# Infini-attention with a channel MLP on one core: the memory read as two 64-row products, dimensions as rows

## The chip, the cores and the metric

The kernel runs on one core of a Trainium2 chip. The time is what the device takes for one execution, in microseconds (us), as the median of several executions. All input and output is float32 in device memory, and one launch does everything. The engines are named as in the profile: PE is TensorE (matrix products; PEld is its loading of weights), DVE is VectorE, ACT is ScalarE, POOL is GpSimd, and SP issues DMAs. Products are written to PSUM, which has eight banks of 128 rows by 512 float32 columns.

## The reference

The input x (2048 tokens, 512 features) is normalised by rows to xn. The output is x + A(xn) + B(xn), where B is a channel MLP (normalise again, 512 to 1792, tanh-approximated GELU, 1792 to 512) and A is an attention of 32 heads of 16 dimensions, in four segments of 512 tokens, with a memory that is carried from segment to segment:

```
for s in range(N):
    qs, ks, vs = q[:, :, s], k[:, :, s], v[:, :, s]
    a_dot = softmax(qs @ ks.T * scale + mask) @ vs
    pq = phi(qs)                                   # where(t > 0, t + 1, exp(t))
    num = einsum("bhld,bhde->bhle", pq, M)
    den = einsum("bhld,bhd->bhl", pq, z)[..., None] + 1e-6
    outs.append(g * (num / den) + (1.0 - g) * a_dot)
    pk = phi(ks)
    M = M + einsum("bhld,bhle->bhde", pk, vs)
    z = z + einsum("bhld->bhd", pk)
```

The part that matters here is the **memory read**: num, den, their quotient and the gate g. M starts as zero, so only segments 1 to 3 need it.

## The kernel before

**Units.** The attention is worked in 16 units: four segments of 512 tokens by four groups of 8 heads (128 features). Unit i is segment i // 4 and group i % 4. For each unit the projections of q and k (`qk_proj`, three f16 products per float32 product, L586) come out with the features as rows and the 512 tokens as columns. Scores are formed twice: once to find row maxima (`m_job`, matrix products L740, maxima on DVE at L747) and once for the softmax (`s_job`, products L782, exponentials on ACT at L789). Both use 48 or 50 rows of the array per product, and always issue two products as a pair: one on rows 0 to 63 and one on rows 64 to 127 (`r = slice(64 * b, ...)`). `pv` (L816) multiplies by the values with float32 operands, four products side by side on 32 columns each. `o_norm` divides, adds the memory's share `ame` (L849, on POOL) and splits the result into two f16 halves for the output projection (L951). The MLP's products are L586 (first layer, `d_job`) and L931 (second layer); they are interleaved with the units.

**The memory read of one unit** (12 units have one) is three steps. `z_cols` (L670, L673, DVE) spreads the group's 128x32 store of M into a block-diagonal 128x128 matrix and z into 128x8, so `mx` has 136 columns. `a_mem` multiplies phi(q) by it, four times 128 tokens (L681), with phi(q) as the stationary operand: tokens become rows, and the four products fill parts of two banks. DVE then divides: denominators (L684), `reciprocal` on 128x32 (L685), gate and scale (L686, `gr` holds the gates of all heads in all rows), and the quotient into `rc` (L689). `a_turn` turns the quotient back to features as rows with four float32 transposes (L696) and copies it on ACT (L698) into `ame`.

**What sets the order.** Nothing is scheduled at run time. The string `ORDER` names, character by character, the stream whose next job is issued; `streams()` builds the streams, `plan()` walks the string and puts in a load of ACT's function table where the next job needs another one, and `CALL` maps a job to its function. Each engine runs its own jobs in that order. The string `BANKS` gives the PSUM bank of each new `dense()` tile in the same way. A bank can be written again only when the last reader of its earlier tile is done, so both strings decide who waits for whom.

## Time and profile before

| | before |
|---|---|
| median of 3 runs | 690.43 us (689.94 to 692.02) |
| span of the profiled execution | 690.7 us |
| PE busy | 680.1 us (98%), 5787 products |
| DVE busy | 498.9 us (72%), 1613 instructions |
| ACT busy | 471.4 us (68%), 877 instructions |
| POOL busy | 346.4 us (50%), 574 instructions |
| granted TensorE clock, mean | 0.999 of full speed |
| DMA | 55.83 MB, mean 81 GB/s |

The profiled execution's span, from its first to its last instruction, is 0.2 us from the median of the timed runs, so terms worked out from the trace can be set against the median directly. Busy times of PE come from records whose ends are modelled: consecutive products overlap in them, and a busy PE is not an array at its peak. Where exact array time is wanted, the chain that ended last gives it better, since it counts from one start to the next.

### The profile page before, as it was taken

The page shows a single profiled execution, that of the slowest core. Times are in us where ns is not written, and L with a number is a line of the kernel's source. Part 1 is how long each engine was busy: PE and PEld are TensorE (multiplying, and loading weights), DVE is VectorE, ACT ScalarE, POOL GpSimd, SP SyncE. Part 2 cuts the span into 40 slices and gives each one's busy share as a digit, 9 for nine tenths or more (in the row PEclk, how much of TensorE's full clock was granted, in tenths as well). Part 3 has the DMA queues.
Part 4 walks back from the last instruction along what each step waited for, and adds up shares of the span by engine and source line. Part 5 has one row for each costly group of instructions (what it writes and reads, how often), then busy time and mean ns, then how long its engine had stood idle before and what let it go on. Part 6 is the DMA issues. An engine that isn't in the chain of part 4 may idle for free.

```text
span 690.7 us, 15732 instructions
## 1 busy us (share of the span) xinstructions
PE 680.1 (98%) x5787; PEld 394.6 (57%) x5787; DVE 498.9 (72%) x1613; ACT 471.4 (68%) x877; POOL 346.4 (50%) x574
## 2 busy tenths in 40 slices
PE   8999999999999999999999999999999999999997
PEld 6764565656644565665555555566565446565543
DVE  5789888986796669676695875878468565787622
ACT  4578898897765578578836838556956554777960
POOL 5576587663525444373545344534372425365652
PEclk9999999999999999999999999999999999999999
DMA  9788433203320342312222133231411222420101
GB/s 267 230 199 218 113 91 105 79 2 91 81 49 16 87 108 55 95 47 72 70 70 57 31 79 86 57 85 39 99 35 56 69 65 61 107 65 2 33 1 61
DMA packets 52889, 55.83 MB, mean 81 GB/s; under 512 B 4990, under 2 KB 41868, under 8 KB 52812
## 3 DMA queue, kind: packets, MB, share of 16 engines
q1 hardware_dynamic: 50508, 50.64, 26.8%
q0 software_dynamic: 2304, 4.20, 3.8%
q8 instruction: 45, 0.74, 0.5%
q14 instruction: 32, 0.26, 0.1%
HBM read 37.77 MB, written 17.05 MB: 79 GB/s over the span
## 4 chain that ended last, share of the span: by engine, by line
PE 87%; DVE 8%; DMA 2%; issue 1%; SPq 1%; POOL 1%; ACT 0%; DVEq 0%
PE dense L586 35%; PE dense L931 20%; PE dense L816 10%; PE dense L951 6%; PE dense L782 6%; PE dense L740 5%; DVE dense L747 4%; PE dense L681 2%; PE dense L696 1%; DVE mc L747 1%; PE dense L564 1%; DMA pt<-in_A_wv_dram 1%; PE dense L651 1%; DMA qst<-md 1%; PE dense L382 0%
## 5 line engine op out<-in xcount | busy, mean ns | idle before, releaser
L747 DVE CUSTOM_DVE_ANT_0 dense<-dense,mask 128x384 f32<-128x384 f32 (+3 forms) x512 | 234.0, 528 | 33.9 <-PE dense L740 33.6
L789 ACT ACTIVATE pt<-dense,qkcs 128x512 f32<-128x512 f32 (+1 forms) x384 | 204.2, 628 | 46.3 <-PE dense L782 46.2
L931 PE MATMUL dense<-w2s,hT 128*128 128x512 f16 x672 | 166.3, 380 | 0.2 <-DVE hT L884 0.2
L586 PE MATMUL dense<-xnT,w1s 128*128 128x256 f16 x1344 | 160.2, 273 | 0.3 <-DVE mc L747 0.3
L803 POOL TENSOR_SCALAR_AFFINE_SELECT pt<-pt 128x256 f32<-128x256 f32 x256 | 99.4, 422 | 108.2 <-ACT pt L789 107.8
L586 PEld LDWEIGHTS <-w1s 128*128 128x128 f16 x1344 | 129.6, 98 | 29.1 <-issue 6.2
L905 POOL TENSOR_TENSOR hT<-hh,hT 128x512 f16<-128x512 f32 x64 | 67.6, 1057 | 83.6 <-ACT hT L903 70.4
L931 PEld LDWEIGHTS <-hT 128*128 128x128 f16 x672 | 61.3, 98 | 68.6 <-issue 13.4
L816 PE MATMUL dense<-pt,vt 128*32 128x512 f32 (+3 forms) x1024 | 78.0, 436 | 0.0
L747 DVE DVE_READ_ACCUMULATOR2_ANT mc<- 128x1 f32 x512 | 74.2, 145 | 0.0
L884 DVE SCALAR_TENSOR_TENSOR hT<-dense,sc,cb 128x512 f32<-128x512 f32 x64 | 43.5, 680 | 33.8 <-PE dense L586 25.2
L847 POOL TENSOR_TENSOR nN<-nN,oT 128x512 f32<-128x512 f32 x16 | 20.9, 1308 | 73.9 <-DVE oT L663 73.9
L901 POOL TENSOR_SCALAR hh<-hT,sc 128x512 f32<-128x512 f32 x64 | 42.5, 664 | 24.1 <-ACT hT L891 15.5
L816 PEld LDWEIGHTS dense<-pt,vt 128*32 128x32 f32 x1024 | 31.1, 109 | 40.7 <-issue 29.4
L782 PE MATMUL dense<-qst,kst 50*128 50x384 f16 (+3 forms) x512 | 52.1, 299 | 1.8 <-DMA qst<-md 1.8
L740 PE MATMUL dense<-kst,qst 48*128 48x384 f16 (+3 forms) x512 | 52.2, 298 | 0.0
L891 ACT ACTIVATE hT<-hT,b1t 128x256 f32<-128x256 f32 x112 | 47.0, 496 | 5.0 <-DVE hT L884 4.6
L903 ACT ACTIVATE hT<-hh 128x512 f16<-128x512 f32 x64 | 37.3, 583 | 14.9 <-POOL hh L901 14.9
L951 PE MATMUL dense<-wos,oT 128*128 128x512 f16 (+2 forms) x204 | 44.0, 367 | 0.8 <-DVE acc L953 0.7
L586 PE MATMUL dense<-xnT,wks 128*128 128x512 f16 (+1 forms) x252 | 44.5, 329 | 0.2 <-DVE mc L747 0.2
L586 PE MATMUL dense<-xnT,wqs 128*128 128x512 f16 (+1 forms) x252 | 44.2, 329 | 0.1
L586 PE MATMUL dense<-wvs,xnT 128*128 128x512 f16 x192 | 43.9, 379 | 0.1
(227 smaller groups left out, 832.0 us busy)
## 6 DMA issues: line engine op xcount, KB each, us to landing
kst<-kd SPq DMA_DIRECT2D x32, 192.0 KB
qst<-qd SPq DMA_DIRECT2D x32, 192.0 KB
qd<-hl SPq DMA_DIRECT2D x36, 128.0 KB
kd<-hl SPq DMA_DIRECT2D x33, 128.0 KB
acc<-in_A_x_dram SPq DMA_DIRECT2D x16, 256.0 KB
acc<-in_B_b_dram POOLq DMA_DIRECT2D x16, 256.0 KB, 4.2
out_dram<-acc SPq DMA_DIRECT2D x15, 256.0 KB
xt<-in_A_x_dram SPq DMA_DIRECT2D x14, 256.0 KB
```

Of the source, the lines that this page charges most:

```text
L586: T.matmul(p, ws(k, a), xs(k, b), start=i == 0, stop=i == 3 * KT - 1)
L740: T.matmul(p[:, o:o + n], stk[i, 0][r, t, P * qb:P * qb + P], stk[i, 1][r, t, :n], start=True, stop=True)
L747: V.tensor_tensor_reduce(p[:, o:o + n], p[:, o:o + n], mask[:, 512 - n:], 1.0, -3e38, OP.add, OP.max, mc[i][:, 4 * b + t, qb:qb + 1])
L782: T.matmul(p[:, o:o + n], stk[i, 1][r, t, P * kb:P * kb + P], stk[i, 0][r, t, P * kb:], start=True, stop=True)
L789: A.activation(pt[i, 4 * b + t][:, OFF[kb]:OFF[kb] + n], p[:, c:c + n], AF.Exp, scale=qkcs[:, 1, i % NG:i % NG + 1])
L803: G.affine_select(v, v, pattern=[[0, 2], [1, P]], compare_op=OP.is_ge, fill=0.0, base=0, channel_multiplier=-1)
L816: T.matmul(p[32 * c:32 * c + 32, P * kb:], vt[s, kb][:, 4 * g + c, 16 * odd:16 * odd + 32], pt[i, 2 * c + odd][:, OFF[kb]:OFF[kb] + LEN[kb ...
L884: V.scalar_tensor_tensor(hz[:, f0:f + 1, :], p[:, :256 * n].rearrange("p (f c) -> p f c", f=n), col(CG + fh), cbt[hf].unsqueeze(1).to_broa ...
L891: A.activation(hz[:, f, :], hz[:, f, :], AF.Gelu_apprx_tanh, bias=b1t[:, fo:fo + 1])
L905: G.tensor_tensor(hT[:, z, 1, :], hht[j, c], hT[:, z, 0, :], op=OP.subtract)
L931: T.matmul(p, t[:, u, P * a:P * a + P], w2s[:, fo, v, :], start=fi == 0 and n == 0, stop=fi == FH - 1 and n == 2)
L951: T.matmul(p[:, c], o[:, u, P * b:P * b + P], wos[:, g, v, c], start=i == 0, stop=i == 3 * NG - 1)
```

## The change

The memory is read with the **dimensions as rows**. `mx` becomes 128x128: columns 0 to 63 hold a block-diagonal copy of M, columns 64 to 127 a copy of z spread over each head's 16 columns, so that the denominator comes out 16 times, once for each dimension of its head. Rows 0 to 63 (four heads) and rows 64 to 127 (the other four) are separate blocks. So the product is two products of 64 rows, 128 columns and 512 tokens, one from each half of the array and each into a bank of its own. phi(q) is now the moving operand. The result has features as rows already: rows 0 to 63 of a bank are numerators, rows 64 to 127 denominators. `z_cols` also multiplies in the gate and the scale (the new column `bg[:, g, 3:4]`; `quad` is a new small constant).

The division moves too. ACT takes the logarithm of the denominators (L689, two instructions of 64x512 with 1e-6 as bias) and the exponential of its negative (L690, 128x512). A new job `a_share` on DVE then refines the reciprocal by one step and multiplies (L697 twice, L698, L700 twice). `a_turn` with its transposes and its copy is gone, and so are `gr` and its preparation in the loading phase. `ame` gets two buffers in place of one `rc` and one `ame`. The job `a_mem` now asks for the table with logarithm and exponential (in `plan`).

```diff
         if s:
             put("mem0", ("Z", i))
             put("mem1", ("Q", i))
-            put("mem2", ("Qt", i))
+            put("mem2", ("Y", i))
...
+        s, g = divmod(i, NG)
+        c = qkcs[:, 0, g:g + 1]
+        if s == 1:
+            V.scalar_tensor_tensor(bg[:, g, 3:4], bg[:, g, 0:1], -1.0, c, op0=OP.mult, op1=OP.mult)
+        mx[i] = sm.tile([P, P], F32, name="mx")
+        V.scalar_tensor_tensor(mx[i][:, :64].rearrange("p (a b c) -> p a b c", a=2, b=2),
+                               mst[:, g, :].rearrange("p (b c) -> p b c", b=2).unsqueeze(1).to_broadcast([P, 2, 2, DH]),
+                               bg[:, g, 3:4],
+                               quad.rearrange("p (a b) -> p a b", a=2).unsqueeze(3).to_broadcast([P, 2, 2, DH]),
+                               op0=OP.mult, op1=OP.mult)
+        V.tensor_scalar(mx[i][:, 64:].rearrange("p (a b) -> p a b", b=DH), quad.unsqueeze(2).to_broadcast([P, 4, DH]),
+                        zst[:, g:g + 1], c, op0=OP.mult, op1=OP.mult)
...
-        ps = [dense()[:, :2 * (P + GH)].rearrange("p (t c) -> p t c", t=2) for b in range(2)]
-        for t in range(4):
-            T.matmul(ps[t // 2][:, t % 2, :], pqt[i, 0][:, P * t:P * t + P], mx[i], start=True, stop=True)
...
-        for t in range(4):
-            T.transpose(p[:, P * t:P * t + P], amt[i][:, P * t:P * t + P], ident)
-        ame[i] = sb.tile([P, 512], F32, name="ame")
-        A.activation(ame[i], p, AF.Copy)
+        mp[i] = [dense() for b in range(2)]
+        R = [slice(64 * b, 64 * b + 64) for b in range(2)]
+        for r, p in zip(R, mp[i]):
+            T.matmul(p, mx[i][r, :], q[r, :], start=True, stop=True)
+        for r, p in zip(R, mp[i]):
+            A.activation(q[r, :], p[64:, :], AF.Ln, bias=tiny[:64])
+        A.activation(q, q, AF.Exp, scale=-1.0)
+
+    def a_share(i):
+        q = pqt[i, 0]
+        t = ame[i] = sb.tile([P, 512], F32, name="ame", bufs=2)
+        R = [slice(64 * b, 64 * b + 64) for b in range(2)]
+        for r, p in zip(R, mp[i]):
+            V.scalar_tensor_tensor(t[r, :], p[64:, :], 1e-6, q[r, :], op0=OP.add, op1=OP.mult)
+        V.scalar_tensor_tensor(q, t, 2.0, q, op0=OP.subtract, op1=OP.mult)
+        for r, p in zip(R, mp[i]):
+            V.tensor_tensor(t[r, :], p[:64, :], q[r, :], op=OP.mult)
```

`ORDER` and `BANKS` are new from their fourth line and their first line on. On TensorE the order is the same, operation for operation, for the first 1036 rows, up to the end of the first values products at about 77 us of the trace; behind that all jobs are put in another sequence. Lines after the edits have moved: L586, L740, L747, L782, L789, L816, L931 and L951 of before are L588, L742, L749, L784, L791, L818, L933 and L953 of the changed kernel.

What stands around a read shows on TensorE at the seventh of the twelve, the one of unit 10. Before, in the middle of the MLP (`w2s` and `w1s` are its weights; `phq` is phi(q)):

```order
L931 LDWEIGHTS hT_126
L931 MATMUL dense_6059<-w2s,hT_126 128x512
L681 MATMUL dense_6190<-mx,phq 128x136 x2
L681 MATMUL dense_6191<-mx,phq 128x136 x2
L586 LDWEIGHTS w1s
L586 MATMUL dense_6202<-xnT,w1s 128x256
```

Now, in the middle of the products for the row maxima (`kst` and `qst` are the stacked keys and queries of a unit):

```order
L742 MATMUL dense_6164<-kst_91,qst_89 128x512
L742 LDWEIGHTS qst_89
L742 MATMUL dense_6165<-kst_91,qst_89 128x512
L687 MATMUL dense_6170<-phq,mx 128x512
L687 MATMUL dense_6171<-phq,mx 128x512
L742 LDWEIGHTS qst_89
L742 MATMUL dense_6177<-kst_91,qst_89 128x384
```

Four products of 136 columns with full rows have become two of 512 columns, and they stand next to products that use the array in 64-row halves as they do. Eight of the twelve reads now have such products on both sides, and three more on one side.

On DVE, at the same read, the division before stood behind an addition of the MLP and ahead of its next eviction (`rd` are denominators):

```order
L935 SCALAR_TENSOR_TENSOR acc<-dense_6059,sc,acc 128x512
L684 TENSOR_SCALAR rd<-dense_6190,qkcs 128x16
L684 TENSOR_SCALAR rd<-dense_6191,qkcs 128x16
L685 RECIPROCAL rd<-rd 128x32
L686 SCALAR_TENSOR_TENSOR rd<-rd,qkcs,gr 128x32
L689 TENSOR_TENSOR rc<-dense_6190,rd 128x256
L689 TENSOR_TENSOR rc<-dense_6191,rd 128x256
L884 SCALAR_TENSOR_TENSOR hT_127<-dense_6202,sc,cb 128x256
```

Now it stands behind six maxima (`ISA` with `mask`, each followed by a read of its result into `mc`), with the bank as the digit behind `dense`:

```order
L749 ISA dense4_6177,mc_6097<-dense4_6177,mask_81 128x128
L749 ISA mc_6097 128x1
L749 ISA dense6_6178,mc_6097<-dense6_6178,mask_81 128x128
L749 ISA mc_6097 128x1
L697 SCALAR_TENSOR_TENSOR ame_6207<-dense5_6170,phq_5853 64x512
L697 SCALAR_TENSOR_TENSOR ame_6207<-dense3_6171,phq_5853 64x512
L698 SCALAR_TENSOR_TENSOR phq_5853<-ame_6207,phq_5853 128x512
L700 TENSOR_TENSOR ame_6207<-dense5_6170,phq_5853 64x512
L700 TENSOR_TENSOR ame_6207<-dense3_6171,phq_5853 64x512
```

The read's two banks, 5 and 3, are held from the products until the last two of these instructions have read the numerators. On TensorE the banks are next written here (row maxima again):

```order
L742 MATMUL dense1_6252<-kst0_91,qst0_89 128x512
L742 LDWEIGHTS qst0_89
L742 MATMUL dense5_6261<-kst0_91,qst0_89 128x384
L742 LDWEIGHTS qst0_89
L742 MATMUL dense3_6262<-kst0_91,qst0_89 128x384
```

Between the read and these rows TensorE has 4 products of the row maxima, 4 of the scores, 9 of the MLP's second layer, 12 of the key projection with 512 columns, and 6 more of the row maxima.

More of the change, by code (lines that the diff above doesn't have):

```diff
@@ L168 @@
+    "541703524137524653724605376240376402537640235174603517460234650213467502"
 )
@@ L304, in w_load @@
             else:
-                stage["1"] = [sb.tile([P, 512], F32, name=t)
-                               for t in ("rc", "ame")]
+                stage["1"] = [sb.tile([P, 512], F32, name="ame", bufs=2) for t in range(2)]
             for j in range(2):
```

86 lines of the change are left out of this document (32 added, 54 removed).

## Prediction

> **What bounds the kernel now.** First the page, for which engine is full, then what that engine waits for, then the chain that ended last.
>
> ```profile
> PE 680.1 (98%) x5787; PEld 394.6 (57%) x5787; DVE 498.9 (72%) x1613; ACT 471.4 (68%) x877; POOL 346.4 (50%) x574
> PE 87%; DVE 8%; DMA 2%; issue 1%; SPq 1%; POOL 1%; ACT 0%; DVEq 0%
> ```
>
> TensorE is full, and 87% of the chain runs over it. The 8% on DVE are not a second bound: the view of TensorE's own waits names hardly any.
>
> ```profile
> PE dense L782 <- DMA qst<-md: 1.8, 2, 1.3
> PE dense L500 <- POOL ident masks.py:199: 1.4, 1, 1.4
> PE dense L951 <- DVE acc L953: 0.7, 1, 0.7
> PE dense L586 <- DVE mc L747: 0.4, 2, 0.3
> ```
>
> The columns are total, times and longest. The first two belong to the start, the third to the end; for a bank that DVE still reads, TensorE stood 0.4 us in the whole run. From about 80 us to the end, then, the time is what TensorE's products take from one start to the next, and a change is worth what it takes out of that sum, as long as it makes no new wait. The chain, shown for two stretches (start, us, what), gives these prices:
>
> ```profile
> 165.39 2.20 PE dense L816 x32
> 167.59 0.76 PE dense L782 x8
> 168.34 0.75 PE dense L931 x3
> 169.10 0.44 PE dense L651 x4
> 169.53 0.93 PE dense L681 x8
> ...
> 207.84 2.59 PE dense L951 x12
> 210.43 0.65 PE dense L931 x3
> 211.07 0.44 PE dense L696 x4
> ...
> 212.48 0.22 PE dense L740 x4
> ```
>
> Three full products of 512 f16 columns take 0.65 us, 0.216 each; behind 64-row products (L782) the same three take 0.75. So **going from one use of the array to another costs 0.10 us**. The four L740 products are two pairs, 384 and 128 columns, one of each pair on rows 0 to 63 and one on 64 to 127: 512 columns per half in 0.22 us, the time of one full product. F16 pairs on the two halves run side by side.
>
> **The change, part by part.**
>
> *Removed on TensorE.* L681 costs 0.93 us per read and L696 0.44, together 1.37. For 12 reads this is 16.4 us.
>
> *Added on TensorE.* Two products of 512 float32 columns. Each float32 product is two passes (the 4 calls of L681 are x8). L681 moves 8 x 136 = 1088 columns in 0.93 us, 0.855 ns per column and pass, so one pass of 512 columns is 0.44 us. If the halves run side by side as the f16 pairs do, the pair costs two passes, **0.88 us**, 10.5 us for 12. No row has a float32 pair on row halves, so this is bounded: from below by 0.88, from above by four passes one after the other, 1.75. I take the lower end, because L816 is the nearer row: float32 too, four products side by side on column strips, 16 products with 1280 columns per strip and two passes. Side by side that is 2560 x 0.855 = 2.19 us; the row has 2.20. Gain so far: 12 x (1.37 - 0.88) = **5.9 us**.
>
> *Changes of the array's use.* Going through TensorE's order, with full products, 64-row pairs and column strips as three kinds, I count 266 changes from one kind to another before and 277 now; the read itself is placed among 64-row pairs, the rest of the new order has more. 11 x 0.10 = **+1.1 us**.
>
> *DVE and ACT.* These rows hold (busy time, then the mean in ns) what goes and what stands nearest to what comes:
>
> ```profile
> L747 DVE CUSTOM_DVE_ANT_0 dense<-dense,mask 128x512 f32<-128x512 f32 x128 | 87.0, 722 | 13.2 <-PE dense L740 13.1
> L747 DVE DVE_READ_ACCUMULATOR2_ANT mc<- 128x1 f32 x512 | 74.2, 145 | 0.0
> L747 DVE CUSTOM_DVE_ANT_0 dense<-dense,mask 128x384 f32<-128x384 f32 x128 | 70.0, 590 | 14.7 <-PE dense L740 14.6
> L747 DVE CUSTOM_DVE_ANT_0 dense<-dense,mask 128x128 f32<-128x128 f32 x128 | 37.3, 335 | 0.0
> L829 DVE SCALAR_TENSOR_TENSOR nN<-dense,bg,nN 128x512 f32<-128x512 f32 x16 | 12.0, 750 | 9.5 <-PE dense L816 9.2 <-POOL hT L905 0.3
> L663 DVE SCALAR_TENSOR_TENSOR oT<-oT,nD 128x512 f32<-128x512 f32 x16 | 11.4, 714 | 0.6
> L689 DVE TENSOR_TENSOR rc<-dense,rd 128x256 f32<-128x256 f32 x24 | 9.1, 419 | 0.4
> L684 DVE TENSOR_SCALAR rd<-dense,qkcs 128x16 f32<-128x16 f32 x24 | 4.8, 228 | 4.5 <-PE dense L681 4.5
> L685 DVE RECIPROCAL rd<-rd 128x32 f32<-128x32 f32 x12 | 4.2, 353 | 0.4
> L686 DVE SCALAR_TENSOR_TENSOR rd<-rd,qkcs,gr 128x32 f32<-128x32 f32 x12 | 3.9, 322 | 0.4
> L824 ACT ACTIVATE nN<-dense,bg 128x512 f32<-128x512 f32 x16 | 11.0, 687 | 29.4 <-PE dense L816 25.7 <-POOL oT L853 3.7
> L658 ACT ACTIVATE nD<-nD 128x512 f32<-128x512 f32 x16 | 10.1, 630 | 0.5
> L698 ACT ACTIVATE ame<-dense 128x512 f32<-128x512 f32 x12 | 7.5, 622 | 11.6 <-POOL nN L849 7.6 <-PE dense L696 3.9
> ```
>
> DVE's division before is 2 x 0.23 + 0.35 + 0.32 + 2 x 0.42 = 2.0 us per read. Now it is two L697 at 0.75 (as L829), L698 at 0.71 (as L663) and two L700. A 64x512 product out of PSUM is not there; L689's 256 columns give 0.42 from below, L829 gives 0.75 from above, and I take 0.69, near L829 for its 512 columns. That is 3.6 us, so 12 x 1.6 = 19 us more on DVE (72% to about 75%). ACT had 0.62 and gets two logarithms at 0.69 (as L824, also out of PSUM with a column operand) and an exponential at 0.63: 2.0 us, 12 x 1.4 = 17 us more (68% to 71%). `z_cols` keeps two small operations per read, and the order has as many loads of ACT's table as before. By itself all this costs nothing: it lies beside TensorE's products, which leave DVE and ACT over a quarter of the span. What it can cost is **bank time**. Before, the read's two banks were free after those 2.0 us on DVE; now they are held for 2.0 us of ACT and then 3.6 of DVE, 5.6 at the least, and longer by what is queued ahead.
>
> The tightest of the twelve is the seventh, shown with the change. Between the read and TensorE's next product into bank 5 stand 9 L933 (1.94 us at 0.216), 12 L588 of 512 columns (2.59), four times 512 columns of 64-row pairs (0.88) and two changes of kind (0.20): 5.6 us. DVE has six maxima ahead of the division: 2 x (0.72 + 0.59 + 0.34) + 6 x 0.15 = 4.2 us. They begin when the products ahead of the read end, 0.9 us before the read does, so the division begins at 3.3. Bank 5 is free at 3.3 + 2 x 0.75 + 0.71 + 0.69 = 6.2, bank 3 at 6.9; TensorE wants them at 5.6 and 5.7. That is a wait of up to 1.2 us, or none if the records' means overstate DVE's pace, as overlapping records do. The other eleven have 6.4 to 14.2 us between read and reuse, counted the same way. I put **+0.5 us** for all twelve, between 0 and 3 (0.25 each).
>
> *The rest.* `gr` leaves three operations of 32 columns out of the loading phase, beside transfers and weight splitting; its order on TensorE is unchanged, so I give it 0. POOL's addition of `ame` now waits for DVE in place of ACT; behind it stand POOL's masks for the softmax, but the order has `a_share` well ahead of it, and `ame` has two buffers. The last unit's end has the same sequence on TensorE: 33 second-layer products behind the last values products, then the output. No DMA is added.
>
> **Sum:** 690.4 - 5.9 + 1.1 + 0.5 = **686.1 us**. The profiled span is 690.7, so the trace needs no correction.
>
> **The rivals.**
>
> *Passes in program order.* If the second product's first pass cannot start before the first product's second pass does, only the middle passes overlap, and the pair costs three passes, 1.31 us. Then 12 x (1.37 - 1.31) = 0.7 is gained, and 690.4 - 0.7 + 1.1 + 0.5 = 691.3: no change. Against it speaks L816, which in such a sequence would need about 16 passes of 320 columns in a row, 4.4 us, and has 2.20. The Trainium skill ("TensorE: Matmul & The Clock Gate", Part 3, "The mechanism") says that products start and end in strict program order. By that rule this rival holds if the two passes of a call stand together in the program; the L816 row speaks for another interleaving.
>
> *Halves one after the other, on the slow side.* If float32 pairs on row halves do not overlap at all, the pair costs 1.75 us: 690.4 + 12 x 0.38 + 1.1 + 0.5 = 696.6. It decides where the pair passes 1.24 us (1.37 less 1.6 / 12); from 1.41 on the kernel is measurably slower. This would also be the case in which the change does not do what it says. For it: no float32 row pair in the trace. Against it: f16 row pairs and float32 column strips both overlap.
>
> *Banks come back late.* If the 5.6 us and DVE's queue make each read wait 0.4 us, 4.8 us replace the 0.5, and the time is 690.4, no change. For it: the seventh read above, and 19 us more on DVE. Against it: the 0.4 us that TensorE waited for DVE before, and eleven reads with more room. The Trainium skill ("TensorEngine Tiling (Array Packing)", "PSUM Bottleneck") warns of this case: tiling speeds up the array and not the emptying of PSUM. The rows agree that emptying grows, from 2.0 to 5.6 us per read; whether it shows depends on the room in the order.
>
> **How the numbers follow.** Side by side with few waits, 686.1 (684 to 688.3): 0.80. Late banks, around 690: 0.10. Program order, 691.3: 0.05. One after the other, 696.6: 0.05. A measurement here tells about 0.3%, 2.1 us, from no change. The first case is faster by more, the next two are within, the last is slower: 0.80, 0.15, 0.05. The range begins at 683.9, with no new waits (685.6) and 1.7 us of old ones gone, and goes to 690.3, into the late banks; the rest of those and the last two cases stay out.
>
> **What would show it.** Right: L687 in the chain at about 0.88 us per read, starts of the two products within some tens of ns, no L696, TensorE's waits for DVE and ACT still below 2 us, DVE near 518 us and ACT near 488 busy. Wrong: a pair of 1.3 or 1.75 us; waits of 64-row products for L700; or a start or end of the run that is longer, which I took as unchanged.

## The result, and the profile after

| | before | after |
|---|---|---|
| median time | 690.37 us (689.94 to 692.02, 4 runs) | 697.71 us (697.01 to 699.42, 4 runs) |
| ratio | | 1.0104, 95% interval 1.0086 to 1.0121 |
| span of the profiled execution | 690.7 us | 696.4 us (its own time: 698.07) |
| granted TensorE clock, mean | 0.999 | 0.997 |

The change makes the kernel 7.3 us **slower**. The prediction was 686.1 us, so 11.6 us are missing. The page of the changed kernel, busy times and shares of the chain that ended last:

```profile
PE 680.2 (98%) x5691; PEld 384.0 (55%) x5691; DVE 525.7 (75%) x1603; ACT 489.3 (70%) x900; POOL 348.4 (50%) x575
PE 71%; ACT 10%; DVE 9%; POOL 3%; DMA 3%; issue 3%; SPq 1%; POOLq 0%; ACTq 0%; DVEq 0%
```

TensorE's busy share has not moved, which shows how little that number says. The chain has: 16 points went from TensorE to ScalarE, POOL and the others. First the read itself, on the timeline of TensorE (start, us, what):

```profile
171.40 0.39 PE L784 MATMUL dense<-qst,kst 50*128 50x512 f16 x2
171.63 1.02 PE L687 MATMUL dense<-phq,mx 64*128 64x512 f32 x4
172.49 0.33 PE L784 MATMUL dense<-qst,kst 50*128 50x384 f16 x2
```

The four passes of the two products go from 171.63 to the next product at 172.49: **0.86 us, side by side**. Six of the twelve reads take that; the other six take 0.91 to 1.06, changes of the array's use among it, and all twelve 10.9. The operations behind it, from the view of single lines (durations in ns: least, median, most):

```profile
L689 ACT ACTIVATE phq<-dense,tiny x24: 683/685/686, 173.7 to 663.3; 64x512 f32<-64x512 f32 x24
L690 ACT ACTIVATE phq<-phq x12: 629/630/632, 175.1 to 664.0; 128x512 f32<-128x512 f32 x12
L697 DVE SCALAR_TENSOR_TENSOR ame<-dense,phq x24: 692/694/696, 175.8 to 665.4; 64x512 f32<-64x512 f32 x24
L698 DVE SCALAR_TENSOR_TENSOR phq<-ame,phq x12: 691/693/769, 177.2 to 666.1; 128x512 f32<-128x512 f32 x12
L700 DVE TENSOR_TENSOR ame<-dense,phq x24: 681/683/685, 178.0 to 667.6; 64x512 f32<-64x512 f32 x24
```

None is above its estimate, so the read's own operations are not what took longer. TensorE's waits (total, times, longest) say more:

```profile
PE dense L784 <- DVE hT L886: 2.7, 1, 2.7
...
PE dense L588 <- DVE phk L639: 1.4, 2, 1.0
...
PE dense L784 <- DVE mc L749: 0.6, 1, 0.6
...
PE dense L588 <- DVE ame L700: 0.3, 1, 0.3
...
PE dense L687 <- ACT pt L791: 0.2, 1, 0.2
```

The largest is a single wait of 2.7 us for the MLP's eviction L886. It is at 104.5 us; **the first read is at 171.6**. For the banks of a read (L700) TensorE waits 0.3 us here.

**A measure for the rest.** Give every product the price that the prediction read from the chain (0.216 us for 512 f16 columns; a float32 product has two passes; products side by side count once; 0.10 us for a change of kind), and add them up in TensorE's order. What a product starts later than this sum is its *lag*: all waiting so far, all slowness of the clock, and whatever a price has too small. The sums are 668.0 us before and 663.1 after: 4.9 less, and the prediction had 5.9 - 1.1 = 4.8. The lag (us), worked out so from the profiled execution of each kernel, at some points of the span:

```
                                  at 60   100   120   140   300   end
before                              9.1  11.9  12.5  12.9  14.4  18.8
after                               9.1  10.0  15.1  15.9  18.9  29.4
```

Of the 10.6 us by which it grew, 4.5 come between 100 and 120 us (5.1 after, 0.6 before), -1.9 ahead of that (a wait for the row maxima's DMA at 68 us that the profiled execution of before has), and 8.0 behind it, in many small pieces. The two spans lie 5.7 us apart and the medians 7.3, since the profiled execution of before is among its slow ones (see below); so at the medians the lag grew by some 1.6 us more.

The chain of the changed kernel through the first place (start, us, what):

```profile
91.95 1.31 PE dense L588 x12
...
94.87 1.28 ACT L1022
96.15 0.01 issue
96.16 0.64 ACT nD L658
96.80 0.02 issue
96.82 0.64 ACT nD L659
97.47 0.02 issue
97.49 2.06 DVE oT L663
...
101.03 1.17 DVE w2s L448
102.20 1.56 DVE w1s L448
103.76 0.66 DVE hT L886
104.43 0.61 DVE xnT L570
105.03 0.04 issue
105.08 0.38 PE dense L784 x3
105.45 4.39 PE dense L588 x24
```

ScalarE loads a function table, then works the reciprocal of unit 0; VectorE waits for it with the refinement (L663, L664) and has two weight splits (L448) behind that, and only then the eviction L886 whose bank TensorE wants. The 24 products at the end take 4.39 us; 12 of the same at 91.95 us take 1.31, so 24 should take 2.62. The windows of 100 to 112 us (length, then busy time and count of PE, PEld, DVE, ACT and POOL, then the granted clock, the DMA share and GB/s), first before:

```profile
100.00:104.50 4.50, 4.50 (x34) 2.61 (x33) 2.92 (x4) 4.47 (x9) 3.82 (x6) 1.00 0.96 200
104.50:108.00 3.50, 3.50 (x29) 2.07 (x31) 2.74 (x6) 3.50 (x9) 2.81 (x6) 1.00 0.54 132
```

and after:

```profile
100.00:104.50 4.50, 1.80 (x12) 0.52 (x11) 4.50 (x5) 3.62 (x7) 4.40 (x4) 1.00 1.02 237
104.50:108.00 3.50, 3.28 (x21) 2.18 (x21) 3.25 (x9) 3.15 (x8) 3.01 (x9) 0.65 0.19 63
108.00:112.00 4.00, 4.00 (x31) 2.12 (x33) 1.90 (x4) 3.28 (x7) 3.18 (x6) 0.88 0.52 166
```

TensorE is idle for 2.7 of 4.5 us (the **hole**) while VectorE is busy throughout, and **behind the hole the clock falls** to 0.65 and 0.88: 0.35 x 3.5 + 0.12 x 4 = 1.7 us more. These two are means over the windows: from 105.6 to 109.0 us the granted clock is 0.50, and 1.00 before and after.

### The profile page after: what moved, and what is told of

It is laid out like the page before. It is cut to its first block, busy times and chain, and to the rows that moved or that the text cites. A ratio compares the mean times of both kernels' runs of the same rounds, so it can differ in the third digit from the quotient of the medians.

```text
span 696.4 us, 15541 instructions
## 1 busy us (share of the span) xinstructions
PE 680.2 (98%) x5691; PEld 384.0 (55%) x5691; DVE 525.7 (75%) x1603; ACT 489.3 (70%) x900; POOL 348.4 (50%) x575
## 4 chain that ended last, share of the span: by engine, by line
PE 71%; ACT 10%; DVE 9%; POOL 3%; DMA 3%; issue 3%; SPq 1%; POOLq 0%; ACTq 0%; DVEq 0%
PE dense L588 30%; PE dense L933 15%; PE dense L818 9%; PE dense L953 5%; PE dense L784 5%; PE dense L742 4%; ACT pt L791 3%; DVE dense L749 2%; PE dense L687 1%; DMA md<-mhl 1%; ACT hT L893 1%; ACT L1022 1%; ACT phq L689 1%; ACT L893 1%; DMA pt<-in_A_wv_dram 1%
## 5 line engine op out<-in xcount | busy, mean ns | idle before, releaser
L749 DVE CUSTOM_DVE_ANT_0 dense<-dense,mask 128x384 f32<-128x384 f32 (+3 forms) x512 | 233.8, 524 | 30.2 <-PE dense L742 27.9
L791 ACT ACTIVATE pt<-dense,qkcs 128x512 f32<-128x512 f32 (+1 forms) x384 | 203.9, 627 | 38.1 <-PE dense L784 37.7
L933 PE MATMUL dense<-w2s,hT 128*128 128x512 f16 x672 | 166.2, 380 | 0.0
L588 PE MATMUL dense<-xnT,w1s 128*128 128x256 f16 x1344 | 162.4, 275 | 0.3
L805 POOL TENSOR_SCALAR_AFFINE_SELECT pt<-pt 128x256 f32<-128x256 f32 x256 | 101.1, 426 | 111.2 <-ACT pt L791 111.0
L588 PEld LDWEIGHTS <-w1s 128*128 128x128 f16 x1344 | 130.7, 99 | 31.0 <-issue 6.1
L933 PEld LDWEIGHTS <-hT 128*128 128x128 f16 x672 | 60.6, 98 | 70.0 <-issue 16.0
L818 PE MATMUL dense<-pt,vt 128*32 128x512 f32 (+3 forms) x1024 | 78.7, 436 | 0.0
L749 DVE DVE_READ_ACCUMULATOR2_ANT mc<- 128x1 f32 x512 | 71.9, 140 | 0.0
L886 DVE SCALAR_TENSOR_TENSOR hT<-dense,sc,cb 128x512 f32<-128x512 f32 x64 | 43.5, 680 | 21.2 <-PE dense L588 20.3
L784 PE MATMUL dense<-qst,kst 50*128 50x384 f16 (+3 forms) x512 | 54.5, 299 | 3.9 <-DVE hT L886 2.7
L742 PE MATMUL dense<-kst,qst 48*128 48x384 f16 (+3 forms) x512 | 55.2, 298 | 1.1 <-DMA qst<-qd 0.4
L818 PEld LDWEIGHTS dense<-pt,vt 128*32 128x32 f32 x1024 | 32.3, 109 | 42.4 <-issue 29.9
L588 PE MATMUL dense<-wvs,xnT 128*128 128x512 f16 x192 | 44.1, 379 | 1.1 <-DVE phk L639 1.0
L588 PE MATMUL dense<-xnT,wks 128*128 128x512 f16 (+1 forms) x252 | 44.4, 329 | 0.5 <-DVE ame L700 0.3
L588 PE MATMUL dense<-xnT,wqs 128*128 128x512 f16 (+1 forms) x252 | 44.2, 329 | 0.4 <-DVE phk L639 0.4
L953 PE MATMUL dense<-wos,oT 128*128 128x512 f16 (+2 forms) x204 | 43.5, 367 | 0.8 <-DVE acc L955 0.7
L905 ACT ACTIVATE hT<-hh 128x512 f16<-128x512 f32 x64 | 37.1, 580 | 10.1 <-POOL hh L903 10.1
```

Of the source, the lines that this page charges most:

```text
L588: T.matmul(p, ws(k, a), xs(k, b), start=i == 0, stop=i == 3 * KT - 1)
L742: T.matmul(p[:, o:o + n], stk[i, 0][r, t, P * qb:P * qb + P], stk[i, 1][r, t, :n], start=True, stop=True)
L749: V.tensor_tensor_reduce(p[:, o:o + n], p[:, o:o + n], mask[:, 512 - n:], 1.0, -3e38, OP.add, OP.max, mc[i][:, 4 * b + t, qb:qb + 1])
L784: T.matmul(p[:, o:o + n], stk[i, 1][r, t, P * kb:P * kb + P], stk[i, 0][r, t, P * kb:], start=True, stop=True)
L791: A.activation(pt[i, 4 * b + t][:, OFF[kb]:OFF[kb] + n], p[:, c:c + n], AF.Exp, scale=qkcs[:, 1, i % NG:i % NG + 1])
L805: G.affine_select(v, v, pattern=[[0, 2], [1, P]], compare_op=OP.is_ge, fill=0.0, base=0, channel_multiplier=-1)
```

## Experiments

Theory A: the new order (with its bank table) costs, read or no read. Theory B: the read's extra work on VectorE and ScalarE costs. Jobs are named as `plan()` yields them: `S`, `M`, `D`, `e`, `T`, `Tw`, `O`, `Xt`, `ws` are score, maximum, first-layer, second-layer and projection jobs, phi, `o_norm`, transposes of normalised tokens, and weight splits. `Q`, `Y` and `Qt` are the read, `a_share` and `a_turn`. The runs e6, e3b, e4b and e9 to e15 also have a `BANKS` made anew from a trace.

### First round: the hole, the two halves of the change, the refinement

**e1_splits_later**

```diff
-("ws", "2b", 3, 0), ("ws", "1b", 5, 0), ("D", 1, 2), ("ws", "1b", 6, 0), ("D", 1, 3), ("ws", "2b", 4, 0)
+("D", 1, 2), ("D", 1, 3)
...
 ("S", 1, 4)
+("ws", "2b", 3, 0), ("ws", "1b", 5, 0), ("ws", "1b", 6, 0), ("ws", "2b", 4, 0)
```

> The changed kernel with four weight-split jobs (two of VectorE, two of GpSimd) moved some 14 jobs down the order, behind the first score jobs of unit 1, so that VectorE reaches the reader of the bank that TensorE waits for at 104.5 us earlier. Theory A (the loss sits mostly in the new order of the loading phase: a 3 us hole in TensorE near 105 us and the lower clock behind it): the hole shrinks below 1 us, the clock stays near 1.00 there, and the time falls by 4 to 5 us, to 692.5-694. Theory B (the loss is spread over the program because the new read loads VectorE more, +27 us of busy time): the time stays within 1 us of 697.7.

Measured: 702.53 us (1.0164, 1.0131 to 1.0197). A miss. The waits of TensorE say why:

```profile
PE dense L588 <- ACT w1s L447: 3.5, 1, 3.5
```

The hole moved on to 107.4 us: a first-layer job there needs the very weights whose split I had put off.

**e3_old_order_new_read**: `ORDER` of before with the new read; `a_share` stands 7 jobs behind the read, with the transposes gone, and two of the twelve reads stand 7 jobs earlier.

```diff
 ("Q", i)
+("Y", i)
...
-("Qt", i)
```

> The new read in the ORDER OF BEFORE: the read's job stands where it stood (two of twelve 7 jobs earlier), its VectorE part 7 jobs behind it, the transposes gone; banks as before, except 19 of 952 that the longer hold makes change. Theory A (the new order is what costs): 685-688 us, faster than before (690.4), since the array saves the 5 us that the traces show and no hole opens at 105 us. Theory B (the read's extra VectorE work makes banks late wherever it stands): 693-697 us.

**e4_new_order_old_read**: the kernel before with the `ORDER` of after; the transposes stand 12 or more jobs behind the read, and one read ten jobs later than after.

```diff
 ("Q", i)
...
-("Y", i)
+("Qt", i)
```

> The old read (128-column products, division, four transposes of the quotient) in the NEW ORDER: read where the new one stands (two of twelve some jobs later), its transposes 12 or more jobs behind it, banks as after save for 12 of 964. Theory A: the hole near 105 us with the low clock behind it is there as after, and the time is 694-697 us. Theory B: the order does no harm, VectorE has the lighter read: 690-692 us.

Measured: 750.29 and 740.05 us (1.0864 and 1.0709). Neither theory had that. The old order with the new read waits for the read's banks:

```profile
PE dense L742 <- DVE ame L700: 17.2, 8, 5.7
PE dense L784 <- DVE ame L700: 6.3, 4, 3.5
```

and the new order with the old read waits for the transposes' bank, but has the hole of 105 us as well, with nothing of the new read in it:

```profile
PE dense L586 <- ACT ame L698: 10.7, 3, 5.6
PE dense L782 <- ACT ame L698: 9.2, 5, 3.1
...
PE dense L782 <- DVE hT L884: 2.7, 1, 2.7
```

What follows: the hole needs no new read; it comes with the new order and its bank table. As a comparison of orders the pair was spoiled, since the few bank numbers that I had to change were badly chosen.

**e5_no_refinement**

```diff
-        for r, p in zip(R, mp[i]):
-            V.scalar_tensor_tensor(t[r, :], p[64:, :], 1e-6, q[r, :], op0=OP.add, op1=OP.mult)
-        V.scalar_tensor_tensor(q, t, 2.0, q, op0=OP.subtract, op1=OP.mult)
```

> The changed kernel without the refinement of the reciprocal (both passes of L697 and L698 are left out: the quotient uses exp(-ln) alone), so that VectorE's work per read falls from five instructions to two, some 2 us times 12 = 26 us of VectorE, and the banks of a read come free earlier. Theory A: the time falls by no more than 1 us (696.5-698). Theory B: it falls by 4-6 us, to 692-694, since VectorE is back at the load it had before.

Measured: 697.76 us (1.0099, 1.0084 to 1.0114). VectorE's busy time fell from 525.7 to 501.1 us, and the time not at all. **Theory B falls for VectorE**, within about a microsecond: in the profiled execution the clock behind the hole stayed low for longer (0.52 and 0.56 in the two windows, for 0.65 and 0.88), which can hide a small gain.

### Second round: the bank table

For every result tile I set the program's order against the trace, to find the moment at which its bank's last reader ended; this is my own working and stands in no view. In the kernel before, the bank chosen is at every tight place the one that came free first. After, the tile at 104.5 us takes a bank that comes free as TensorE starts, while another had been free for 3.07 us.

**e7_two_bank_swaps**: two exchanges of bank numbers, from the 145th tile on; the first changed line:

```diff
-    "54026153740153726051372654017362015743201657340165734017365407136507136524136524013642501367421537460521374052"
+    "54026153740153726051372654017362017534201675430167543015467305146705146723146723014632701465321745360721453072"
```

> The changed kernel, its order untouched, with two exchanges of bank numbers from the 145th and the 147th result tile on (the two at which TensorE waits at 104.5 and 105.1 us): by the trace of the changed kernel the bank chosen there comes free only as TensorE starts, another one had been free for 3.07 us. Theory C (the table of banks, not the order and not the read, opens the hole near 105 us): the 2.9 us wait goes, the clock stays near 1.00 in 104-112 us, and the time falls by 4.5-6 us to 692-693. Theory A (the new order makes VectorE late there, whichever bank is taken): the wait moves to the next tile, and the time stays within 1.5 us of 697.7.

Measured: 697.56 us (1.0102, 1.0077 to 1.0126), 695.56 to 699.45. The 3.07 us were slack only because TensorE had stood: the next tile waited 2.80 us at 104.4 us. In this execution the clock did not fall behind the hole:

```profile
100.00:104.50 4.50, 1.87 (x14) 0.76 (x14) 4.50 (x5) 4.50 (x9) 4.40 (x4) 1.00 0.86 241
104.50:108.00 3.50, 3.29 (x30) 2.69 (x30) 3.40 (x10) 3.41 (x9) 3.50 (x10) 1.00 0.19 60
```

and its span was 693.8 us, 2.6 less than after; but the other three runs took 697.5 to 699.5, at a mean clock of 0.996 to 0.997 for the 1.000 of this one. At 0.003 of 696 us, some 2 us of that difference go with the clock and not with the swaps.

**e6_banks_by_trace**: `BANKS` new throughout, by the rule above.

> The changed kernel, its order untouched, with the whole table of banks made anew: each result tile takes, of the banks that are free in program order, the one that came free first by the trace of the changed kernel. Against the two swaps alone it mends four more places (404, 435, 469 and 470 us: 1.4 us of waits become slack). Theory C: 690.5-692.5 us. Theory A: 696-698 us.

Measured: 695.27 us (1.0066, 1.0050 to 1.0083). 2.4 us come back, less than half of what theory C wanted. The hole broke up into waits of 1.01, 0.54, 0.52, 0.36 and 0.31 us, and the clock stayed at 1.00. The order is untouched here, so the bank table has a part in the hole.

**e3b_old_order_new_read_banks** and **e4b_new_order_old_read_banks**: the two mixed kernels with `BANKS` by the same rule, from their own traces.

> The new read in the old order again, with the table of banks made anew by the trace of the first such run (750 us), in which sixteen waits, 40 us together, were for a bank still held by a read or by its neighbours while another had been free for 0.5 to 7 us. Theory C (what the bank table costs was hidden in that run): the time falls by 35-55 us, to 695-715. If the old order itself cannot hold the new read (its read stands too near its consumers): it stays above 725 us.

> The old read in the new order again, with the table of banks made anew by the trace of the first such run (740 us), in which thirteen waits were for a bank that another one could have replaced. Theory C: the time falls by 35-45 us, to 695-705, and the hole near 105 us is gone. If the new order cannot hold the old read: it stays above 725 us.

Measured: 728.37 us (1.0551) and 714.46 us (1.0344); 22 and 26 us come back, not 35 or more. So **each order fits its own read**: the old one leaves no room for a read that holds two banks some 6 us long, and the new one is no order for the old read either.

### Third round: no read at all, a light read, the hole once more

**f2a_after_no_read** and **f2b_before_no_read**: the same cut in both kernels.

```diff
-                G.tensor_tensor(n, n, ame[i], op=OP.add)
+                G.tensor_tensor(n, n, nd[i][2], op=OP.add)
...
-        "Q": a_mem, "Y": a_share,
+        "Q": lambda i: None, "Y": lambda i: None,
```

> The changed kernel with the memory read left out altogether (the scaled factors, the two products, the logarithm and exponential, the quotient); the sum that takes it in adds another tile of the same size, so GpSimd's work is as before, and the banks of the read are struck from the table. To be set against the same cut of the kernel before (next run). The array work that goes is 12 x 0.86 = 10.3 us here and 12 x 1.37 = 16.4 us there. Theory A (the new order with its banks is the price, whether there is a read in it or not): 685-688 us, some 10-13 us above the cut kernel before. Theory D (the new read's own work on ScalarE and VectorE and the banks that it holds are the price): 674-678, within 4 us of the cut kernel before.

> The kernel before with the memory read left out in the same way (factors, products, division, transposes and their copy). By the rows of its trace the array loses 12 x (0.93 + 0.44) = 16.4 us: 673-675 us under either theory; it is the mark for the run before this one.

Measured: 692.01 us (1.0021, 1.0009 to 1.0033) and 680.34 us (0.9851, 0.9828 to 0.9873). Without any read the new order is 11.7 us slower (1.70% of 690, give or take 0.26 points, 1.8 us, by the two intervals), as theory A had it. Both times as such are misses: the rows give the old read 16.4 us of array time and the new one 10.3, and only 10.1 and 5.7 came off. Either order loses part of the gain to waiting when its read is gone. This splits the result: the old read was worth 690.4 - 680.3 = 10.1 us, the new one 697.7 - 692.0 = 5.7, so **the new read saves 4.4 us, and the new order takes 11.7**, 7.3 together. That the two add up to 7.3 is so by construction; the 4.4 is good to some 2 us by the three intervals. One reserve: an order made for a read is judged here without it, and the waits that this opens are in both figures. The hole is there without a read:

```profile
PE dense L784 <- DVE hT L886: 2.7, 1, 2.7
```

**f1b_after_light_read**: e5's edit, and with it

```diff
-        for r, p in zip(R, mp[i]):
-            A.activation(q[r, :], p[64:, :], AF.Ln, bias=tiny[:64])
-        A.activation(q, q, AF.Exp, scale=-1.0)
...
-            V.tensor_tensor(t[r, :], p[:64, :], q[r, :], op=OP.mult)
+            V.scalar_tensor_tensor(t[r, :], p[:64, :], 0.0, q[r, :], op0=OP.mult, op1=OP.mult)
```

> The changed kernel with the reciprocal left out of the read: no logarithm, no exponential, no refinement (L690 to L692 and both L697, L698), and the last two instructions multiply by zero, so that the read adds nothing; its products, its place and its banks stay. ScalarE is spared some 2 us and VectorE 2 us per read. Theory A: 695-697 us. Theory D: 690-692 us.

Measured: 696.22 us (1.0084, 1.0065 to 1.0103), 1.5 less than after, as theory A had it. The reciprocal's 24 us on each of two engines may cost somewhat more: in the profiled executions the clock behind the hole was at 0.50 for 6.8 us here and for 3.4 after, which is worth 1.7 us, and behind 120 us the lag grows by 3.0 less (table below).

**e9_newton_later**

```diff
-("O", 0, 2), ("ws", "2b", 3, 0)
 ("ws", "1b", 5, 0), ("D", 1, 2)
...
-("ws", "2b", 4, 0)
...
 ("Xt", 1, 0, 1)
+("O", 0, 2), ("ws", "2b", 3, 0), ("ws", "2b", 4, 0)
```

> The changed kernel with three jobs moved down the order, behind the last evictions that TensorE waits for near 104 us: the refinement of unit 0's reciprocal (L663, L664: 2.05 + 1.53 us on VectorE there, behind ScalarE's table load) and two weight-split jobs (L448, 1.17 us on VectorE; one of GpSimd); the table of banks is made anew by the trace of the changed kernel. VectorE then reaches the eviction L886 some 3 us earlier. Theory A (order): no wait over 1 us and a clock near 1.00 in 100-112 us, and a time of 691-693.5 us, below the 695.3 that the new table of banks alone gave. If the wait there has another cause: 695 us or more.

Measured: 695.34 us (1.0078, 1.0053 to 1.0103), no better than the banks alone. VectorE was early now, and TensorE waited for ScalarE at 105.8 us:

```profile
PE dense L784 <- ACT pt L791: 2.3, 1, 2.3
```

The new order issues five score jobs of unit 1 with one projection among them; the old one had a projection and two first-layer jobs there. Their twelve exponentials take ScalarE 6.4 us (2.40, 1.29 and 2.72 on its timeline of after), their products TensorE some 1.1 (0.22 a job), so the banks run out, it seems, whichever other engine is relieved.

### Last rounds: where in the order

**e10_scores_spread**, on top of e9:

```diff
 ("S", 1, 2)
-("S", 1, 3), ("S", 1, 4)
...
 ("D", 1, 5), ("e", 2, 0, 0)
+("S", 1, 3), ("S", 1, 4)
```

> The run before it (refinement later) with one edit more: two of the five score jobs of unit 1 that follow each other stand ten jobs later, behind three projection jobs that need nothing of ScalarE (some 3.2 us of TensorE's work), and the banks by the trace of the run before it. There TensorE waited 2.5 us at 105.8 us for ScalarE's exponentials of just these score jobs. Theory A (order: the readers of the banks are booked up, and the order gives TensorE nothing else to do there): no wait over 1 us in 95-120 us, and 691-693 us. If the hole is of another kind, it opens a few us later and the time stays at 695 or more.

Measured: 699.53 us (1.0076 to 1.0147 around 1.0112). A miss: the wait came back at 111.2 us, 2.53 us long, for L886.

**e11_old_loading_order**: the first 411 jobs in the old order, then those that remain in the new one.

> The changed kernel with the OLD order for its first 411 jobs (to some 128 us, the loading phase; no memory read lies in it) and the NEW order, with the new read, from there on (the two orders have done the same jobs at the cut, but for three); banks by the two traces. The lag of TensorE behind its array work grew by 0.6 us from 100 to 120 us before and by 5.1 us after. Theory A: the loading part goes back to what it was, 692-693.5 us, and what is left above the 686.1 that the array work alone would give (some 6 us) sits behind 128 us. If the loss belongs to the read: 696-698.

Measured: 696.44 us (1.0074, 1.0050 to 1.0098). The stretch that it was about is mended (its window of 100 to 104.5 us); the second fence is the longest of TensorE's waits:

```profile
100.00:104.50 4.50, 4.50 (x41) 3.29 (x40) 3.03 (x3) 4.47 (x10) 3.13 (x5) 1.00 0.77 156
```

```profile
PE dense L566 <- POOL xt L539: 2.9, 1, 2.9
```

The wait is new, at the seam, at 132.9 us, with a clock of 0.79 from 132 to 140 us. By the time alone this is the answer "the loss belongs to the read" (696-698); only the lag, below, shows that the stretch itself was mended.

**e12_old_loading_seam** puts the transposes at the seam (where the old order goes over into the new one) later, and one job of VectorE (`Z`) behind its neighbours, and **e13_seam_light_read** is e12 with f1b's edit:

```diff
-("D", 3, 2), ("H", 1, 2, 1), ("Xt", 1, 1, 0), ("X", 1, 1, 4), ("N", 3), ("D", 3, 3), ("Xt", 1, 1, 1), ("H", 1, 2, 2), ("e", 2, 1, 4), ("e", 2, 1, 5)
+("D", 3, 2), ("N", 3), ("D", 3, 3), ("X", 1, 1, 4), ("e", 2, 1, 4), ("e", 2, 1, 5), ("H", 1, 2, 1), ("Xt", 1, 1, 0), ("Xt", 1, 1, 1), ("H", 1, 2, 2)
```

> The run before it (old order for the first 411 jobs) with the seam mended: there TensorE waited 3.0 us at 132.9 us for GpSimd's normalisation of a token tile (L539), a wait that neither order alone has. Seventeen jobs behind the cut are put in another sequence, so that five pieces of TensorE's work stand ahead of the two transposes that need that tile; banks by the trace of that run. Theory A (order): no wait over 1 us from 60 to 300 us, a lag of about 12 us at 140 us (15.9 in the run before, 12.9 in the kernel before), and 691.5-693.5 us; what then remains above 686.1 us is behind 140 us. If the time stays at 695 or more, the loading phase was not what cost.

> The same order and banks with the light read: logarithm, exponential and refinement left out, the last two instructions multiply by zero. If the waits behind 140 us come from the work that the new read puts on ScalarE and VectorE, it falls by 4 us or more below the run before this one; if they come from the order there, by 2 us or less (1.5 us was the difference in the changed kernel's own order).

Measured: 696.14 us (1.0088, 1.0070 to 1.0106) and 693.86 us (1.0043, 1.0027 to 1.0059). At the seam 2.17 us of wait remained. The time is in the range that was to speak against the loading phase (695 or more); again only the lag speaks for it. The light read gains 2.3 us, between the two answers.

**e14_seam_closed**, e12 with this edit, and **e15_three_waits**, e14 with the second one and with one more product put ahead at each of two later waits:

```diff
 ("X", 1, 1, 2)
+("X", 1, 1, 3), ("X", 1, 1, 4)
...
-("Xt", 1, 1, 0), ("Xt", 1, 1, 1), ("H", 1, 2, 2), ("O", 1, 2)
+("H", 1, 2, 2), ("O", 1, 2), ("Xt", 1, 1, 0), ("Xt", 1, 1, 1)
 ("S", 2, 0)
```

```diff
-("pv", 7, 1, 1)
...
 ("M", 8, 4)
+("pv", 7, 1, 1), ("pv", 7, 1, 2), ("PV", 7, 1)
 ("V", 2, 0)
```

> As the last run but one (old loading order, then the new order with the new read), with the wait at the seam attacked from its cause: there TensorE still waited 2.17 us at 135.3 us for GpSimd's normalisation (L539), with the clock at 0.91 from 120 to 140 us. Both normalisations now stand right behind the statistics they need, ahead of another GpSimd job, and the two transposes four jobs later. Theory A (order of the loading phase): no wait over 1 us from 60 to 300 us, a lag of 11.5-12.5 us at 140 us, and 691.5-693 us. If the time stays at 695 or more, the loading phase was not what cost.

> The same with three of the later waits for VectorE covered by moved TensorE work (351.6 us: 1.05; 446.6: 0.50; 592.7: 0.50): three parts of a score-value product, one projection and one MLP product are put ahead of the job that waits. Theory A: 1-2 us below the run before this one, 690-692, about the kernel before. If waits only move on to the next job: no change, within 0.5 us of it.

Measured: 698.41 us (1.0109, 1.0087 to 1.0132) and 702.23 us (1.0166, 1.0135 to 1.0197). Two misses of one kind, and e14's time too lies where it was to speak against the loading phase. In e14 the wait moved 3 us on, from 135.3 to 138.1 us, to score jobs; its waits and the windows there:

```profile
PE dense L784 <- DVE xnT L570: 2.8, 1, 2.8
```

```profile
137.00:141.00 4.00, 2.89 (x15) 1.73 (x15) 2.04 (x3) 4.00 (x8) 3.52 (x5) 0.79 0.01 2
141.00:145.00 4.00, 4.00 (x34) 2.51 (x33) 2.81 (x11) 2.48 (x6) 0.03 (x1) 0.78 0.00 0
```

In e15 the three products that were to cover a wait of 1.05 us made the next one 2.9 us long, since the eviction behind them (L832) came later:

```profile
PE dense L588 <- DVE nD L832: 2.9, 1, 2.9
```

The lag of these kernels (us), worked out as above:

```
                                  at 60   100   120   140   300   end
before                              9.1  11.9  12.5  12.9  14.4  18.8
f2b, before without read            9.0   9.8  10.3  10.7  12.9  23.3
after                               9.1  10.0  15.1  15.9  18.9  29.4
f2a, after without read             9.4  12.1  16.8  17.6  21.8  34.9
f1b, after with a light read        9.4  10.4  16.5  17.3  19.5  27.8
e6, banks by the trace              8.8  10.2  13.0  13.9  16.3  26.2
e12, old order up to 128 us         9.1   9.9  10.9  14.9  17.2  27.1
```

Up to 120 us e12 lags 4.2 us less than after, and e11 and e14 do so too (11.1 and 11.0): the loading phase of the new order costs that by the lag, and it was the old order that gave it back. Each of these kernels then lost 4 to 5 us between 120 and 140 us, at a seam of my making. From 140 us to the end the lag grows by 5.9 us before, 13.5 after, 12.2 in e12 and 10.5 in f1b; without a read it grows by 12.6 in the old order (f2b) and 17.3 in the new one (f2a).

## Why the prediction was wrong

- **The pair of products**: predicted 0.88 us, side by side; measured 0.86, and 10.9 for all twelve with the changes of use that some of them bring. Both rivals about it (1.31 in program order, 1.75 one after the other) are refuted by the starts: at every read the two first passes start 3 to 7 ns apart, and the two second ones 0.43 to 0.54 us later, side by side again.
- **Transposes and changes of use**: -5.9 + 1.1 = -4.8 predicted; the priced sums differ by -4.9. These sums use the prediction's own prices, so they confirm the count and not the size. The count leaves out 16 single products on one column strip (L753, now L755): with them there would be 296 changes before and 291 now, and the 1.1 would be -0.5. What was measured is the read's whole share, with its banks: 4.4 us saved (good to some 2) for 5.9 - 0.5 = 5.4. That agrees.
- **The durations on VectorE and ScalarE**: 0.75, 0.71, 0.69, 0.69 and 0.63 predicted; 0.69, 0.69, 0.68, 0.69 and 0.63 measured. ScalarE's busy time is 489.3 us for 488. VectorE's is 525.7 for 518; some 3 to 4 us of the difference are instructions that ran longer beside POOL (below).
- **Bank waits of the read**: +0.5 predicted, 0 to 3. For L700 the view of waits has 0.3 us; without logarithm, exponential and refinement the time falls by 1.5 us (f1b) and 2.3 (e13 against e12), and the lag behind 120 us by 3.0 (f1b). The term was too small, and its bounds held, the upper one just. The refinement alone costs nothing that shows (e5). The 0.4 us that TensorE had waited for VectorE before leave out 1.0 us for L384 at 35 us, which both kernels have.
- **The step that failed is "The rest"**, with its 0, and the sentence that put on record that behind 77 us "all jobs are put in another sequence". The sum priced that sequence with 1.1 us, for the changes of the array's use, and looked for waits only at the twelve reads. It took the other waits of the new order to be those of the old one. Cut free of the read, the new order costs 11.7 us, give or take 1.8: 1.1 by the prediction's price, and 10.6 for which the sum had no term. (The 10.6 us of lag further up are another sum, with the reads and their waits in it; that the two figures are alike is an accident.) No rival had it either; the slow-side rival's 696.6 is near the result by accident, for its mechanism did not occur.
- **Where they sit**: the two kernels without a read differ in lag by 11.6 us at the end. Of these, 2.3 come ahead of 100 us (most of them waits for DMAs ahead of 77 us, where the order is the same), 4.2 between 100 and 120 us (a hole of 2.9 us, and the clock behind it), and 5.1 behind 120 us. With their reads the kernels differ by -1.9, 4.5 and 8.0 in the same stretches, the last in dozens of waits between 0.1 and 1.05 us. For the loading phase the lag shows the cause: with the old order there, there is no hole (e11, e12, e14), and a bank table by the trace takes half of the excess away too (e6: the lag grows by 2.8 there, for 5.1 after and 0.6 before). The times of these runs hardly show it, since e11, e12 and e14 each lost 4 to 5 us at their seam. Behind 120 us the new bank table gives 1.1 us of lag back (e6), and the read's work has the 1.5 to 3.0 above; **the remainder is not traced to a cause**. Every attempt to mend a wait by hand moved it on (e1, e7, e9, e10, e12, e14, e15), and no kernel here that has the whole new read beats the one before.
- **The correction of the trace**: "needs no correction" was 1.7 us off. Where a run lists both, its time is 1.6 to 2.7 us above its span, mostly 1.7 (698.07 and 696.4 us after; 680.53 and 678.8 for f2b). So the profiled execution of before probably took 692.4 us, among its slowest, and its 1.8 us of DMA waits at 68 us are more than most other traces have there (0.3 after). This does not touch the sum, whose terms are differences.

## What to carry to other kernels

When a change brings a new hand-made order, the order is a change of its own, with a price of its own: lay the work of VectorE and ScalarE against TensorE's in every stretch that is reordered, not only where the edited operation stands, and look for runs of jobs whose readers are slower than the products (five score jobs in a row here). Cut the edited operation out of both kernels and time them: two runs told the price of the order from that of the operation, to some 2 us, which the eight runs before them had not. An order, a bank table and an operation that were fitted together do not come apart: the four mixtures of one kernel's read and the other's order were all slower than either kernel.

## What the runs showed of the hardware

**A hole costs more than its length.** Its length is counted here as in the lag, some 0.1 to 0.3 us above the view of waits. Outside the four mixtures of read and order, and with e4's hole at 105 us, there are fifteen holes of 2.1 to 3.7 us (fourteen before 145 us and one at 359 in e15). Behind thirteen of them the granted clock was 0.50, for 3.4 us (eleven) or 6.8 (e5 and f1b); two had no fall (e7, 2.80 us; e9, 2.53). The four mixtures have nineteen more, of 2.2 to 5.9 us: fifteen came with such a fall, four without, one of them 3.1 us long (e4, 491 us). One wait of 1.40 and 0.31 us close together (e10, 69 us) was followed by 0.50 from 71 to 73 us, while waits of 1.2 to 1.6 us at the same place in before, e9, e14 and f2a were not. So the fall is likely behind a hole, and not certain. This fits the scatter of kernels with a hole: 695.6 to 699.5 us for e7, 694.7 to 696.3 for e6, which has none. The Trainium skill ("TensorE: Matmul & The Clock Gate", "Why this matters for your kernels") advises to keep idle gaps below about 3 us; here gaps of 2.2 and 2.5 us were already followed by a low clock, and one of 3.1 us was not.

**VectorE beside POOL.** An instruction of VectorE that reads and writes SBUF alone can be held up while POOL works. After the change 29 of them ran over 0.1 us longer than is usual for their line and shape: all 29 were among the 119 that ran beside a POOL instruction, none among the 109 that did not, and none of the 846 that use PSUM was so long (reads of an accumulator are left out). On VectorE's timeline of after:

```profile
351.24 1.39 DVE L633 TENSOR_SCALAR phk<-phk,qksc 128x512 f32<-128x512 f32 x1
352.67 0.69 DVE L639 SCALAR_TENSOR_TENSOR phk<-dense,phk 128x512 f32<-128x512 f32 x1
```

and on POOL's (in brackets, how long it was idle before, and for whom):

```profile
351.20 1.15 POOL L907 TENSOR_TENSOR hT<-hh,hT 128x512 f16<-128x512 f32 x1 [2.17 <-ACT hT L905]
```

L633 takes 0.48 us where nothing disturbs it; here it ends 0.28 us after POOL's instruction, and TensorE's wait of 1.0 us for L639 at 353 us is behind it. L663 in the hole is another (2.05 us for 0.68). Over the whole run, what VectorE's instructions take beyond the usual time of their form (by over 0.1 us each) adds up to some 10 us before and 13 to 14 after. The Trainium skill ("SBUF — State Buffer", "SBUF: two separate sides") says that the two engines share a pair of ports, which one of them holds for a whole instruction while the other stands, if VectorE's instruction uses both ports in a fast mode or reads two operands from SBUF while the other reads there too. The rows fit this in the main: L663 reads two operands from SBUF; L633, with one, ends 0.28 us behind POOL's instruction, less than the 0.48 us that it takes alone, so a part of it had been done.
